# Attention with a learned distance bias and two gated layers on one core: raw rows loaded later, another grouping of the first layer, no conversions in step 0

## The chip, the cores and the metric

The kernel runs on one core of a Trainium2 chip. TensorE (PE in the profile; PEld are its weight loads) multiplies matrices, VectorE (DVE), ScalarE (ACT) and GpSimd (POOL) do the elementwise work, SyncE (SP) issues transfers between HBM and the on-chip memory. The metric is the device time of one execution in microseconds: 643.84 us, the median of three runs of the kernel before (643.73 to 643.98).

## The reference

```python
# attention: B, H, S, D = 2, 8, 576, 64
scores = q @ k.T / 8
x = log1p(|i - j|) / log1p(max(i, 1))            # of positions i, j
bias = relu(x[..., None] @ w1 + b1) @ w2         # 32 hidden, 8 heads
attn = softmax(scores + bias); a = attn @ v      # to 1152 tokens x 512
# first gated layer, 512 -> 1536 -> 512
y = (sigmoid(a @ w_gate) * (a @ w_val)) @ w_out
# second gated layer, after an RMS norm
yn = y / sqrt(mean(y * y) + 1e-6) * g
out = (silu(yn @ w_gate2) * (yn @ w_val2)) @ w_out2
```

## The kernel before, in words

Each engine runs its instructions in the order in which the program emits them; the program writes that order out by hand, as a list of actions for each turn of its loops.

**The bias.** The bias of 16 rows of positions (index T, 36 of them) is made from a table of logarithms: `bias_h` (L222) computes four hidden tiles `ht` on VectorE, ScalarE or GpSimd, `bias_mm` (L240) multiplies them by the second weights on TensorE and scales the sums into a row block `be` on ScalarE (in part on VectorE, L269), `bias_end` (L271) mirrors it and stores it to HBM (`bias_d`, on SyncE). Before the attention loop `bias_step` (L295) runs 18 times (L721) for the first 16 values of T; these are the first two tiles of positions (tile 2, then tile 1), eight values each. `load_bias` (L318) loads a block `bt` of a finished tile back, for two heads at a time; `feed_bias` (L339) does so for all units up to a number, as far as their tile is stored.

**The attention.** There are 36 units: a tile of 128 rows, a pair of heads `hp` and a batch b (the last four hold both batches). The first four are tile 2 with pairs 0, 0, 1, 1. `load_raw` (L162) loads q and k of one pair and batch in two halves of 288 KB, one per head; the first pair's and second pair's second halves go through ScalarE's queue, all others through SyncE's. In the kernel before the first two pairs (eight halves) are loaded ahead of all bias work (L192). For unit n, turn n of the loop at L732 takes the scores and bias together with their minimum (`reduce_min`, L370, VectorE), the exponential (`expo`, L389, ScalarE), the normalisation; three turns later come the transposes (L419) and the products with v (L454, `pv`).

**The gated layers.** The 1536 hidden values are 12 blocks f, the tokens three chunks c of 384. A step is one (layer, group, chunk, block); `GROUPS` says how many blocks form a group. Within a group the order is chunk by chunk, and for each chunk all blocks of the group. There are 72 steps. In turn s of the loop at L808 the program emits `gate_val(s)` (two products of 12 matmuls, `gv`, then the sigmoid `sg` on ScalarE, the product `g` on VectorE, its rounded copy `gh` on ScalarE), conversion steps, `low_part(s)` (`gl`, VectorE), `out_mm(s-2)` (12 matmuls into an accumulator `acc`) and more conversion steps. gate_val(0) is emitted earlier, in turn 36 of the attention loop. When a chunk's last block of a group is done, `collect` (L589) brings the accumulator's four parts to `part`: in a layer's first group two copies each on ScalarE and VectorE (L597, L595), in later ones four additions on VectorE (L593). The next chunk's first `out_mm` (the head) reuses that accumulator and waits for it.

**The weights** (72 pieces: gate, value and output of each block and layer) come as 512 KB transfers and are converted to two 32-bit parts, in four steps each (`piece_step`, L516): steps 0, 1, 2 and 3 have one VectorE instruction each (L522, L531, L535, L540), steps 0 and 2 have ScalarE instructions as well, step 1 an addition on GpSimd (L532). `advance(limit, micro)` emits up to `micro` such steps. In the gated loop `pace(s)` (L679) chooses how many: at least 5, up to 8 if a piece's first use comes soon. From turn 22 of the attention loop one conversion step is emitted per turn (`C`), and in the turns from 36 to 39 three.

**The norm** of the second layer runs for each chunk in four stages, one per step (`norm_stage`, L617), from the step in which the chunk's last `out_mm` of layer one is emitted; stage 3 ends with four scalings (L658) and four subtractions (L662) on VectorE, and the second layer's first step on that chunk needs them.

Of the kernel before, what the change touches and what calls it, by code (L numbers as in the profile page):

```python
# [17 lines left out]
B, H, S, D = 2, 8, 576, 64  # L18
# [5 lines left out]
CH = 384  # L24
NCH = NT // CH

GROUPS = ((2, 3, 3, 4), (4, 4, 4))
RING, EARLY, MORE = 24, 7, 7
TL = 3
WARM = 11  # L30
# [53 lines left out]
def groups_of(it):  # L84
    a, r = BLK[it]
    return range(a // 16, (a + r) // 16)
# [11 lines left out]
def fused_kernel(ctx: ExitStack, tc: tile.TileContext, qk, vp, tab, pcol, invp, prm, wts, rg, out):  # L98
    nc = tc.nc
# [58 lines left out]
    def half(b, h):  # L158
        x = (h + b) % 2 * 64
        return slice(x, x + 64)  # L160

    def load_raw(b, hp):  # L162
        t = wk.tile([128, 2, S], F32, tag=f"raw{hp // 2}", name=f"raw{b}{hp}", bufs=4)
        raws[b, hp] = t
        for h in range(2):
            r = half(b, h)
            q = nc.scalar if h and hp < 2 else nc.sync
            q.dma_start(t[r], qk[b, hp][:, r, h].rearrange("w p s -> p w s"))

    vs = {}  # L170
# [15 lines left out]
    def drain(q, k=99):  # L186
        while q and k:
            q.pop(0)()
            k -= 1

    nc.sync.dma_start(w1l[:, PARTS[1]], tab[:, PARTS[1]])
    for hp in range(2):  # L192
        for b in range(B):
            load_raw(b, hp)
    nc.sync.dma_start(w1l[:, PARTS[2]], tab[:, PARTS[2]])
    nc.sync.dma_start(w1l[:, PARTS[3]], tab[:, PARTS[3]])
    nc.gpsimd.tensor_scalar(nbpc, bpr, prms[:, 1:2], -1.0, op0=ALU.mult, op1=ALU.mult)
# [5 lines left out]
    def table(i):  # L203
        x = w1l[:, PARTS[i]]
        nc.vector.tensor_scalar(x, x, prms[:, 0:1], None, op0=ALU.mult)
# [89 lines left out]
    def bias_step(more=True):  # L295
        bias_rest()
        m, e = mq[:1], eq[:1]
        if hq and more:
            T = hq.pop(0)
            bias_h(T, *BIAS_H[GORDER.index(T)])  # L300
            mq.append(T)
        for T in m:
            bias_mm(mq.pop(0))
            eq.append(T)
        for T in e:
            bias_end(eq.pop(0))
        if eq and GORDER.index(eq[0]) < AT_ONCE:
            bias_end(eq.pop(0))
# [6 lines left out]
    NU = len(UNITS)  # L315
    st = {}

    def load_bias(n):  # L318
        b, hp, it = UNITS[n]
        bt = wk.tile([128, 2, S], F32, tag="bt", name=f"bt{n}", bufs=3)  # L320

        w = bias_width(it)
        r = rows_of(it)
        flat = bias_d[it].rearrange("a w -> (a w)")
        for h in range(2 if b is None else 1):
            o = r - 1 + (2 * hp + h) * w
            rows = flat[o : o + r * (H * w - 1)].rearrange("(i k) -> i k", k=H * w - 1)
            if b is None:
                nc.sync.dma_start(bt[h * 64 : h * 64 + 64, 0], rows[:, :S])
            else:  # L330
                nc.sync.dma_start(bt, rows[:, : 2 * w].rearrange("i (a k) -> i a k", a=2)[:, :, :S])
        st[n, "bt"] = bt
        if b is not None:
            st[n + 1, "bt"] = bt
# [4 lines left out]
    def feed_bias(last, wait=0):  # L339
        while ahead and ahead[0] <= last:  # L340
            it = UNITS[ahead[0]][2]
            seen = stored[: len(stored) - wait]
            if any(T not in seen for T in groups_of(it)):
                return
            load_bias(ahead.pop(0))
# [131 lines left out]
    def members(l, g):  # L477
        a = sum(GROUPS[l][:g])
        return range(a, a + GROUPS[l][g])

    STEPS = [
        (l, g, c, f) for l in range(2) for g in range(len(GROUPS[l])) for c in range(NCH) for f in members(l, g)
    ]
# [88 lines left out]
    def out_mm(s):  # L572
# [3 lines left out]
        head, last = f == members(l, g)[0], f == members(l, g)[-1]  # L576
        final = g == len(GROUPS[l]) - 1
        if head:
# [93 lines left out]
    def deadline(k):  # L672
        return USES[PIECES[k][:2]][0]

    def closing(s):
        return 0 <= s < NS - 1 and STEPS[s][:3] != STEPS[s + 1][:3]


    def pace(s):  # L679
        need, begun = 5, done[0] + done[1] + done[2] - 3 * done[3]  # L680
        for k in range(done[3], min(NPC, done[3] + RING)):
            todo = 4 * (k + 1 - done[3]) - begun
            need = max(need, -(-todo // max(1, deadline(k) - s - 1)))
        return min(need, 8)
# [36 lines left out]
    for i in range(PRE + 2):  # L721
        bias_step(i < PRE)
        if i == 3:
            table(1)
        if i == 9:
            feed_bias(2)
            qk_mm(0)
        if i == 12:
            table(2)
            table(3)  # L730

    for n in range(NU + TL + 1):  # L732
        if n == NU:
            attn.close()
            open_ring("me", range(EARLY, EARLY + MORE), "left")
        ev = []
        turn = (n - TL + 1) % 2
        on_dve = (1,) if n < NBIAS or n >= NU else (1,3,4)

        def evac(i):  # L740
            if len(ev) > i:
                if i in on_dve:
                    nc.vector.tensor_copy(*ev[i])
                else:
                    nc.scalar.activation(*ev[i], AF.Copy)

        def load_new():
            if n in LOADR:
                load_raw(*LOADR[n])
            if n in LOADV:  # L750
                load_v(*LOADV[n])
            if n in LASTV:
                load_last(*LASTV[n])

        live = n < NU
        nb = BSTEPS.get(n, 0)
        acts = {
            "M0": lambda: live and reduce_min(n, 0),
            "M1": lambda: live and reduce_min(n, 1),
            "X0": lambda: live and expo(n, 0),  # L760
            "X1": lambda: live and expo(n, 1),
            "T": lambda: 0 <= n - TL < NU and ev.extend(transp(n - TL)),
            "E3": lambda: evac(3),
            "E4": lambda: evac(4),
            "E0": lambda: evac(0),
            "E1": lambda: evac(1),
            "E2": lambda: evac(2),
            "N": lambda: 0 <= n - 1 < NU and normal(n - 1),
            "C": lambda: n >= NBIAS + LAG and advance(EARLY if live else EARLY + MORE, 1 if live else 2),
            "B": lambda: live and feed_bias(n + 4),  # L770
            "D": bias_rest,
            "A": lambda: nb > 1 and bias_step(),
            "c": lambda: nb > 2 and bias_step(),
            "b": lambda: nb and bias_step(),
            "L": load_new,
            "Q": lambda: n + 1 < NU and qk_mm(n + 1),
            "P0": lambda: drain(peq, 5),
            "P1": lambda: drain(peq, 5),
            "V": lambda: 0 <= n - TL < NU and [pv(UNITS[n - TL + i]) for i in range(2)],
        }  # L780
        for x in ORDERS["bias" if n < NBIAS else "late" if live else "end"][turn].split():
            acts[x]()
        if n == NBIAS - 1:
            assert not eq
            prod.close()
            open_ring("mc", range(EARLY), "right")
            fetch()
        if n >= NU:
            advance(EARLY + MORE, 1)
        if n == NU:  # L790
            while (0, 0, 1) not in wp:
                advance(EARLY + MORE, 1)
            gate_val(0)
# [14 lines left out]
    for s in range(NS + 2):  # L808
        while s < NS and (STEPS[s][0], STEPS[s][3], 1) not in wp:
            advance(done[3] + 1, 1)  # L810
        if 0 < s < NS:
            gate_val(s)
        micro = pace(s)
        if any(q[0] <= s for q in norm_queue):
            micro = min(micro, 2)

        parts = (0, micro) if closing(s - 2) else (micro // 2, micro - micro // 2)
        for half in range(2):
            k = done[3]
            if k < NPC:  # L820
                lim = k
                while lim < NPC and lim < k + 3 and (lim < RING or released(lim - RING) <= s):
                    lim += 1
                advance(lim, parts[half])
            if half == 0:
                if s < NS and not closing(s - 2):
                    low_part(s)
                if s > 1:
                    l, _, _, f = STEPS[s - 2]
                    while (l, f, 2) not in wp:  # L830
                        advance(done[3] + 1, 1)
                    out_mm(s - 2)
                if closing(s - 2):
                    low_part(s)
                while norm_queue and norm_queue[0][0] <= s:
                    _, c, stage, box = norm_queue.pop(0)
                    norm_stage(c, stage, box)
                    if stage < 3:
                        norm_queue.append([s + 1, c, stage + 1, box])
# [68 lines left out]
```

## Time and profile before

| | before |
|---|---|
| median of three runs | 643.84 us |
| profiled execution | 646.62 us |
| its span, first to last instruction | 644.8 us |
| TensorE busy | 631.2 us |
| VectorE busy | 486.2 us |
| ScalarE busy | 350.9 us |
| GpSimd busy | 214.4 us |
| mean granted TensorE clock | 0.995 |

Times in the rows below are microseconds from the first instruction of that one execution. Bias and attention take the first 175 us; the gated steps follow, some 6.27 us each in the steady state. The span is 1.8 us shorter than the execution, and the execution 2.8 us longer than the median of the runs without a profile.

### The profile page before, as it was taken

To read this page: it belongs to the slowest core of one execution; us is meant where nothing else is said; L and a number is where in the kernel's file an instruction comes from. 1 tells how busy PE (TensorE), PEld (TensorE's weight loads), DVE (VectorE), ACT (ScalarE), POOL (GpSimd) and SP (SyncE) were. 2 spreads that over 40 slices of the span, in tenths; PEclk is the share of its full clock that TensorE was granted. 3 is DMA by queue.
4 is the path that set the end of the run, shared out by engine and by line. 5 is a ranking of instruction groups with operands and counts; after the bars stand their busy time and mean duration, and the time that the engine had idled before them with its cause. 6 is when DMAs were issued, how large, how long until landed. Compare 5 with 4: busy or idle time off the path is not lost.

```text
span 644.8 us, 11729 instructions
## 1 busy us (share of the span) xinstructions
PE 631.2 (98%) x4450; PEld 575.3 (89%) x4450; DVE 486.2 (75%) x954; ACT 350.9 (54%) x745; POOL 214.4 (33%) x237
## 2 busy tenths in 40 slices
PE   9789999999998999999999999999999999999997
PEld 4246767788898999999999999999999999999997
DVE  7898898699869898888987889777877888431322
ACT  5768888988875554455543636444545445111110
POOL 6301777576753332323323221020322423100000
PEclk9999999999999999999999999999999999999999
DMA  8876956754234332343332422121433322000111
GB/s 196 293 250 199 226 187 189 261 151 131 79 94 129 103 110 91 97 132 101 116 95 82 131 65 63 38 67 33 131 99 100 109 87 66 0 1 1 50 49 50
DMA packets 28472, 71.73 MB, mean 111 GB/s; under 512 B 3840, under 2 KB 6912, under 8 KB 28416
## 3 DMA queue, kind: packets, MB, share of 16 engines
q1 hardware_dynamic: 26688, 68.41, 35.2%
q10 hardware_dynamic: 1728, 2.58, 1.4%
q8 instruction: 35, 0.57, 0.4%
q14 instruction: 21, 0.17, 0.1%
HBM read 57.72 MB, written 13.25 MB: 110 GB/s over the span
## 4 chain that ended last, share of the span: by engine, by line
PE 92%; DVE 3%; ACT 2%; DMA 2%; issue 0%; SPq 0%
PE gv L555 47%; PE s L360 6%; PE tp L419 5%; PE pv L454 5%; PE bps L253 4%; DMA bias_d<-be 1%; DVE ht L235 1%; PE pvNone L454 1%; DVE t L370 1%; PE acc122a L585 1%; DMA bt<-bias_d 1%; PE acc102b L585 1%; PE acc100b L585 1%; PE acc121b L585 1%; PE acc101b L585 1%; PE acc120b L585 1%
## 5 line engine op out<-in xcount | busy, mean ns | idle before, releaser
L532 POOL TENSOR_TENSOR ff<-ff,wr 128x512 int32<-128x512 int32 x72 | 113.9, 1582 | 260.0 <-DVE ff L531 132.9
L561 DVE TENSOR_TENSOR g<-gv,sg 128x384 f32<-128x384 f32 x72 | 40.1, 557 | 91.3 <-PE gv L555 77.2
L563 ACT ACTIVATE gh<-g 128x384 fp32r<-128x384 f32 x72 | 37.8, 525 | 99.4 <-DVE g L561 99.4
L555 PE MATMUL gv<-xh,wh 128*128 128x384 f32 x216 | 73.1, 339 | 0.0
L555 PE MATMUL gv<-xl,wh 128*128 128x384 f32 x216 | 72.8, 337 | 0.0
L555 PE MATMUL gv<-xh,wl 128*128 128x384 f32 x216 | 72.8, 337 | 0.0
L555 PE MATMUL gv<-nh,wv 128*128 128x384 f32 x240 | 64.1, 336 | 0.0
L522 DVE TENSOR_SCALAR ff<-wr 128x512 uint32<-128x512 uint32 x72 | 63.4, 881 | 0.0
L389 ACT ACTIVATE p<-t,mn 128x576 f32<-128x576 f32 x72 | 55.4, 769 | 12.7 <-DVE mn L370 12.6
L403 POOL TENSOR_SCALAR p<-p,rs 128x576 f32<-128x576 f32 x60 | 52.0, 879 | 24.3 <-PE tp L419 9.6
L370 DVE CUSTOM_DVE_ANT_0 t<-s,bt 128x576 f32<-128x576 f32 x72 | 51.6, 755 | 10.9 <-PE s L360 7.5
L559 ACT ACTIVATE sg<-gv 128x384 f32<-128x384 f32 x72 | 34.5, 480 | 44.8 <-PE gv L555 44.8
L536 ACT ACTIVATE wh<-ab 128x512 fp32r<-128x512 f32 x42 | 26.5, 632 | 56.2 <-DVE ab L535 55.8
L360 PE MATMUL s<-raw 64*128 64x288 f32 (+1 forms) x320 | 48.5, 432 | 4.1 <-DVE mn L370 4.0
L235 DVE TENSOR_SCALAR ht<-w1l,bpc 128x304 f32<-128x304 f32 (+17 forms) x100 | 51.7, 580 | 0.1
L535 DVE SCALAR_TENSOR_TENSOR ab<-ab,ff 128x512 f32<-128x512 f32 x72 | 49.0, 681 | 3.2 <-POOL ff L532 3.2
L569 DVE TENSOR_TENSOR gl<-g,gh 128x384 fp32r<-128x384 f32 x72 | 45.3, 629 | 7.0 <-ACT gh L563 7.0
L531 DVE SCALAR_TENSOR_TENSOR ff<-wr,ff 128x512 uint32<-128x512 uint32 x72 | 50.3, 699 | 0.0
L555 PE MATMUL gv<-nh,wh 128*128 128x384 f32 x144 | 48.7, 338 | 0.0
L555 PE MATMUL gv<-nl,wh 128*128 128x384 f32 x144 | 48.6, 337 | 0.0
L555 PE MATMUL gv<-nh,wl 128*128 128x384 f32 x144 | 48.6, 337 | 0.0
L525 ACT ACTIVATE wr<-wr 128x512 int32<-128x512 uint32 x72 | 48.2, 669 | 0.0
(423 smaller groups left out, 1578.7 us busy)
## 6 DMA issues: line engine op xcount, KB each, us to landing
wr<-wts SPq DMA_DIRECT2D x72, 512.0 KB, 3.6
bias_d<-be SPq DMA_DIRECT2D x36, 295.5 KB, 5.0
bt<-bias_d SPq DMA_DIRECT2D x16, 576.0 KB, 5.4
raw<-qk SPq DMA_DIRECT2D x12, 288.0 KB, 8.0
v<-vp SPq DMA_DIRECT2D x8, 320.0 KB, 4.1
raw<-qk ACTq DMA_DIRECT2D x4, 288.0 KB, 8.7
bt<-bias_d SPq DMA_DIRECT2D x8, 144.0 KB, 3.3
out<-part SPq DMA_DIRECT2D x6, 192.0 KB, 1.8
```

Source lines behind the costliest of these rows:

```text
L235: nc.vector.tensor_scalar(ht, src, bpc[:, t : t + 1], 0.0, op0=ALU.add, op1=ALU.max)
L360: nc.tensor.matmul(dst[:, hf, :288], raw[r, 0, r0 : r0 + rows], raw[r, 1, cs], start=True, stop=True)
L370: nc.vector.tensor_tensor_reduce(t, sp[:, :, :288], bt[:, 0 if UNITS[n][0] is None else j].rearrange("p (a c) -> p a c", a=2), -SCALE, 3.0e38,
L389: nc.scalar.activation(p[:, j], t.rearrange("p a c -> p (a c)"), AF.Exp, bias=mn[:, j : j + 1], scale=-1.0, accum_out=sm[:, j : j + 1],)
L403: nc.gpsimd.tensor_scalar(p[:, j], p[:, j], rs[:, j : j + 1], 1.0, op0=ALU.mult, op1=ALU.mult)
L522: nc.vector.tensor_scalar(ff, hw, 3, 0x3FFFFFFF, op0=ALU.logical_shift_left, op1=ALU.bitwise_and)
L525: nc.scalar.activation(lw.bitcast(I32), lw, AF.Copy, scale=2.0**-29)
L531: nc.vector.scalar_tensor_tensor(ff, hw, 0xC0000000, ff, op0=ALU.bitwise_and, op1=ALU.bitwise_or)
L532: nc.gpsimd.tensor_tensor(ff.bitcast(I32), ff.bitcast(I32), lw.bitcast(I32), op=ALU.add)
L535: nc.vector.scalar_tensor_tensor(ab, ab, TINY_HI, ff.bitcast(F32), op0=ALU.is_ge, op1=ALU.mult)
L555: nc.tensor.matmul(ps[:, :CH], wt[:, cs], xt[:, cc, :], start=(k == 0), stop=(k == 11))
L569: nc.vector.tensor_tensor(gl, g32, gh.bitcast(F32), op=ALU.subtract)
```

## The change

The first layer's 12 blocks are grouped 2, 2, 2, 3, 3 instead of 2, 3, 3, 4. The second pair's raw rows (four halves) are no longer loaded at the beginning but in the tenth turn of the first bias loop, behind the first bias block and before the second; both their halves go through SyncE's queue. The attention loop has one turn less at its end (n = 39, in which nothing but conversion steps is emitted). In step 0 of the gated loop no conversion steps are emitted.

```diff
-GROUPS = ((2, 3, 3, 4), (4, 4, 4))
+GROUPS = ((2,2,2,3,3), (4, 4, 4))
...
-            q = nc.scalar if h and hp < 2 else nc.sync
+            q = nc.scalar if h and hp < 1 else nc.sync
...
-    for hp in range(2):
-        for b in range(B):
-            load_raw(b, hp)
+    for b in range(B):
+        load_raw(b, 0)
...
         if i == 9:
+            feed_bias(0)
+            load_raw(0, 1)
+            load_raw(1, 1)
             feed_bias(2)
             qk_mm(0)
...
-    for n in range(NU + TL + 1):
+    for n in range(NU + TL):
...
-        micro = pace(s)
+        micro = pace(s) if s else 0
```

## Rows read from the trace of the kernel before

**Rows 1.** The page, part 1: busy time of each engine, share, instructions.
```profile
PE 631.2 (98%) x4450; PEld 575.3 (89%) x4450; DVE 486.2 (75%) x954; ACT 350.9 (54%) x745; POOL 214.4 (33%) x237
```

**Rows 2.** TensorE's waits, whole span: us in total, times, longest.
```profile
PE s L360 <- DVE mn L370: 4.0, 2, 3.1
...
```

**Rows 3.** TensorE's waits from 62 us to the end: all.
```profile
PE acc001a L585 <- ACT part L597: 2.5, 1, 2.5
```

**Rows 4.** Chain that ended last, 15 to 33 us: start, us, what.
```profile
18.16 6.22 DMA bias_d<-be
...
24.46 4.32 DMA bt<-bias_d
...
```

**Rows 5.** VectorE's timeline, 18 to 29 us: start, us, instruction, [idle before].
```profile
22.91 2.77 DVE L235 TENSOR_SCALAR ht<-w1l,bpc 128x368 f32<-128x368 f32 x7
28.80 0.76 DVE L370 CUSTOM_DVE_ANT_0 t<-s,bt 128x576 f32<-128x576 f32 x1 [3.12 <-DMA bt<-bias_d]
```

**Rows 6.** SyncE's waits, 0 to 30 us.
```profile
SPq L287 <- DMA raw<-qk: 5.7, 4, 2.7
...
```

**Rows 7.** SyncE's timeline, 8 to 40 us (issues; us are those of issuing).
```profile
10.14 9.85 SPq L287 DMA_DIRECT2D bias_d<-be  x9
24.46 0.89 SPq L331 DMA_DIRECT2D bt<-bias_d  x2
...
36.70 0.37 SPq L331 DMA_DIRECT2D bt<-bias_d  x1
...
```

**Rows 8.** Windows: us, busy PE, PEld, DVE, ACT, POOL, PEclk, DMA share, GB/s.
```profile
8.00:16.00 8.00, 7.89 (x54) 2.25 (x50) 8.00 (x17) 6.51 (x15) 6.95 (x11) 1.00 1.07 221
...
```

**Rows 9.** ScalarE's timeline, 24.5 to 34.5 us.
```profile
27.62 0.41 ACT L281 ACTIVATE be<-be 128x255 f32<-128x255 f32 x1
29.60 0.77 ACT L389 ACTIVATE p<-t,mn 128x576 f32<-128x576 f32 x1 [1.56 <-DVE mn L370]
...
```

**Rows 10.** VectorE's timeline, 29.4 to 62 us.
```profile
34.36 0.58 DVE L269 TENSOR_SCALAR be<-bps,nip,corr 128x288 f32<-128x288 f32 x1 [0.20 <-PE bps L253]
...
36.09 0.16 DVE L396 TENSOR_SCALAR sm<-sm 128x2 f32<-128x2 f32 x1
...
51.69 0.75 DVE L370 CUSTOM_DVE_ANT_0 t<-s,bt 128x576 f32<-128x576 f32 x1
...
```

**Rows 11.** TensorE's timeline, 205 to 212.5 us.
```profile
207.78 0.57 PE L585 MATMUL acc001a<-gh,wh 128*128 128x384 f32 x1 [2.45 <-ACT part L597]
...
```

**Rows 12.** Windows around that wait, columns as in rows 8.
```profile
203.50:205.30 1.80, 1.80 (x11) 1.50 (x9) 1.80 (x4) 0.49 (x1) 0.00 (x0) 1.00 0.54 98
...
207.80:211.35 3.55, 3.55 (x12) 3.55 (x13) 3.46 (x8) 2.20 (x5) 1.27 (x1) 0.52 0.48 149
...
```

**Rows 13.** Chain that ended last, 170 to 212 us.
```profile
184.17 8.52 PE gv L555 x48
...
201.09 4.26 PE gv L555 x24
...
206.97 0.77 ACT part L597 x2
...
```

**Rows 14.** VectorE's timeline, 179 to 196 us.
```profile
184.77 0.55 DVE L522 TENSOR_SCALAR ff<-wr 128x512 uint32<-128x512 uint32 x1
...
189.36 1.54 DVE L522 TENSOR_SCALAR ff<-wr 128x512 uint32<-128x512 uint32 x1
...
194.54 0.54 DVE L561 TENSOR_TENSOR g<-gv,sg 128x384 f32<-128x384 f32 x1
...
```

**Rows 15.** Windows of three steps each; the highest and lowest of four.
```profile
286.95:305.80 18.85, 18.85 (x110) 18.85 (x110) 16.43 (x26) 9.54 (x19) 6.30 (x4) 1.00 0.39 112
305.80:324.60 18.80, 18.80 (x109) 18.80 (x109) 15.91 (x26) 9.82 (x20) 4.97 (x3) 1.00 0.36 112
```

**Rows 16.** Line 593's instructions: ns min/median/max, first and last start.
```profile
L593 DVE TENSOR_TENSOR part<-acc010a,part x2: 547/552/558, 248.9 to 249.9; 128x384 f32<-128x384 f32 x2
...
```

**Rows 17.** Line 658's instructions, as in rows 16.
```profile
L658 DVE SCALAR_TENSOR_TENSOR part<-part,rgs,rb x12: 606/608/615, 389.1 to 443.6; 128x384 f32<-128x384 f32 x12
...
```

## The prediction

> **What bounds the kernel now.** The page's busy line first: TensorE is busy 631.2 of 644.8 us [rows 1]. No instruction of TensorE is added or removed by the change, so all it can win is inside the other 13.6 us, and it loses wherever it makes TensorE wait anew. So the next view is TensorE's waits. Over the whole span the largest is for the minimum of the scores, 4.0 us in two waits, both in the first 62 us [rows 2]. From 62 us to the end there is one wait only: 2.45 us at the second chunk of the first gated group [rows 3]. These are the two places that the change can touch; behind each I go back along the chain.
>
> *The start.* The chain in order of time shows the last store of the first bias tile under way from 18.16 for 6.22 us, the load of the first bias block from 24.46 for 4.32 us [rows 4], and VectorE, which ended its hidden-layer work at 22.91 + 2.77 = 25.68, idle for 3.12 us until that block landed [rows 5]. SyncE's waits say why the stores were late: four issues of stores waited 5.7 us in all until raw q/k rows had landed [rows 6]. From there to 62 us VectorE paces the kernel (it has hardly a gap, the first later one being 0.20 us [rows 10]), so time won ahead of it is time won at the end.
>
> *The stall.* TensorE stood 2.45 us before the first product of out_mm(2), until ScalarE had copied the first chunk's sums out [rows 11, 13]. Its clock was 1.00 (the 2.4 GHz level) before and 0.52 (near the 1.2 GHz level) for 3.55 us after [rows 12]. The copies were late because sigmoid and product of the gated steps ran late: the 48 matmuls of gate steps 1 and 2 ended at 184.17 + 8.52 = 192.69, so step 1's half ended near 188.4, but VectorE took up its product at 194.54 [rows 13, 14], 6.1 us late. In between it worked on conversions.
>
> **The change part by part.**
>
> *Second pair's raw rows moved.* Eight half loads of 288 KB stood ahead of the stores; four leave. At 221 GB/s, which the chip moved in 8 to 16 us [rows 8], a half takes 294,912 B / 221 GB/s = 1.33 us, so 5.3 us of transfer leave the queue ahead of the stores. What is late next is the stores' own data: nine stores stand before the first bias load in SyncE's order, and the ninth was issued by 10.14 + 9.85 = 19.99 [rows 7]; its data come from VectorE and TensorE, which the loads do not hold. So the bias load issues near 20.0 instead of 24.46. With its 4.32 us [rows 4] it lands at 24.3, and VectorE wants it at 25.68: the 3.12 us go, with 1.4 us of cover.
>
> The next limit is ScalarE: it is busy with bias rows until 27.62 + 0.41 = 28.03 and begins the first exponential at 29.60 [rows 9], so that one comes only 1.56 us sooner. VectorE's first use of it, at 36.09 [rows 10], is some 4 us behind the end of the pair (29.60, two exponentials of 0.77 and a hidden tile, about 32), so this does not pace it. The 0.20 us wait for the second half of a bias row may grow a little, as ScalarE makes one of the hidden tiles ahead of it. Bounds: 1.56 us (ScalarE paces) to 3.12 us (nothing does). I take 2.9, near the upper one, since the VectorE row is the one on the path.
>
> What is added behind: four raw halves on SyncE instead of two on each queue, 4 x 1.33 = 5.3 us of transfer between the first bias block (24.3) and the second, which then lands some 2.7 us on (589,824 B / 221 GB/s), near 32.3. The second pair is first wanted by VectorE after its 36.09 step, less 2.9. Seven stores of the second tile follow; its first bias load, issued at 36.70 [rows 7], slips by about 1 us, while its user stands at 51.69 [rows 10], now 48.8. Both are covered by over 1 and 6 us. If the first cover were gone, the loss would be what is late, up to the gain.
>
> *Rule and row on this order.* The first bias load took 4.32 us although another block and seven stores were issued right behind it [rows 4, 7]. The Trainium skill, "DMA: Bandwidth & Descriptors", section "Queues, rings and completion order", says that one queue's descriptors are consumed in ring order on each DMA engine, while different queues take turns. By that, raw halves on SyncE's own queue stay behind the bias block, as in the sum; had they shared turns with it, the block would land as in the second rival.
>
> *No conversions in step 0, and one loop turn less.* Walking the planner: the last turn (n = 39) emits three conversion steps, step 0 emits five (pace 5). All eight stand ahead of gate step 1's product on VectorE. In the trace this is all between 184.77 + 0.55 = 185.32 and 194.54, 9.2 us, with one low part in it [rows 14]. Without them VectorE does low_part(0) (0.55 us) and is free at about 185.9, before gate step 1 ends (188.4): product 1 moves from 194.54 to about 188.5. Then step 1's conversions run, five as now: c5.2, c6.1, low part, c5.3, c7.0, c6.2 (cK.i is piece_step(K, i)). At about 0.55 us each and one blocked beside GpSimd (1.54 [rows 14]) that is 4.5 us, to about 193.5, so product 2 is 1 us late rather than 7.8. Step 2 takes 4 us, product 3 waits for its gate step, and the copies, two on each engine, follow out_mm(1) at once. That ended at 201.09, where gate step 4 starts [rows 13]; the copies end near 202 and TensorE wants them at 205.3. The wait goes, with 3 us of cover. Weight pieces: step 1 needs piece 4, converted at n = 38; out_mm(1) needs piece 5, now finished in step 1.
>
> Worth: 2.45 us, and the clock. 3.55 us at 0.52 instead of 1.00 lost 3.55 x (1 - 0.52) = 1.7 us [rows 12]; with no idle ahead I let that go too. Bounds: 0 (stall moves to another head), 2.45 (clock falls anyway), 4.15. I take 4.1.
>
> *Groups of 2, 2, 2, 3, 3.* What it gives: weights of hidden blocks 2 to 4 are due in steps 6 and 12, not 6 to 8, so the planner's pace stays at 5 although eight conversion steps are missing; walked with the old groups it would be 7 in step 1 and 6 in steps 2 to 6. What it costs: 15 chunk ends instead of 12, three more with four adds of 0.55 us [rows 16] = 6.6 us of VectorE in all, beside TensorE. Room: in four stretches of three gate steps (18.85 us) VectorE was busy 15.9 to 16.4 [rows 15]. Less four adds of 0.5 us a step is 4.7, so two steps with a chunk end need 2 x 4.7 + 2.1 = 11.5 of 12.55 us. It fits, with 1 us to spare. Adds are done 2.0 us after their first, and the next chunk's first product stands one gate step (4.2 us) behind: no wait. Cost 0; bound 6 us and clock losses (third rival).
>
> The norm of chunk 0 now ends at step 34 (32 before), of chunk 1 at 37 (36), in the same steps as adds. After step 34's gate: adds to +3.7, low part 4.2, four scalings of 0.61 us at 0.53 spacing [rows 17] 6.3, first low half 6.9, the last near 8.4. Gate step 36 starts after out_mm(32), gate step 35 and out_mm(33): 2.1 + 4.2 + 2.1 = 8.4 (12, 24 and 12 matmuls at 4.26 us for 24 [rows 13]), and wants the last low half some 1.6 us later still. Cover 1.5 us; cost 0, bound 3 us.
>
> **Sum.** 2.9 + 4.1 = 7.0 us. The profiled execution took 646.62 us (span 644.8, 1.8 around it), so it would be 639.6; the median of the runs shown is 2.78 us below it, 643.84 - 7.0 = **636.8 us**.
>
> **Rivals.**
> 1. *Only the start wins.* Conversions left out at step 0 come back at once and an accumulator head at steps 4 to 8 waits as long as before: 643.84 - 2.9 = 640.9. For it: VectorE is some 85% busy [rows 15]. Against: it starts 6 us earlier and the pace does not rise.
> 2. *The bias block shares the DMA engines with the raw halves behind it*: 576 + 4 x 288 KB = 1.77 MB at 221 GB/s [rows 8] from 20.0 land near 28.0, so VectorE waits 2.3 of its 3.12 us: the start wins 0.8, the stall 4.1. Time 643.84 - 4.9 = 638.9. Against: [rows 4].
> 3. *Slower: VectorE overruns in the groups of two.* Six chunk ends in a row, steps 9 to 19. If two of the two steps' ten conversions are blocked once more beside GpSimd (1.54 instead of 0.6, 0.94 each [rows 14]), two steps need 13.4 instead of 11.5, each of the six heads waits 0.85 us and pays up to the 1.7 of the clock: 15.3 us. 643.84 - 7.0 + 15.3 = 652.1. It decides from 1.2 us a head. Against: the 1 us to spare.
> 4. *Norm and adds collide at step 36*: 1 to 3 us with the clock, 638.8 at 2.
>
> **How the numbers follow.** Forecast 0.62 (its own range 635.3 to 638.0), rival 1 0.10, rival 2 0.10, rival 3 0.08, rival 4 0.10. The range 634.9 to 641.2 holds the forecast and rivals 1, 2 and 4 but for their tails. 0.2% is 1.3 us, about what can be told from no change. Forecast and rivals 1, 2, 4 are faster; rival 3 is slower in some three quarters of its cases; some tail lies within 0.2%: faster 0.88, same 0.05, slower 0.07.
>
> **What would show it.** VectorE's first score reduction near 25.7 without idle; first bias load issued near 20 and landed before 25.7; no wait of TensorE at acc001a, clock 1.00 around it; product 1 right behind its gate step; no TensorE wait in gate steps 4 to 40. Wrong if any accumulator head of groups 1 to 3 waits, if gate step 36 waits for the norm, or if VectorE still idles at its first reduction.

## The result and the profile after

The kernel after takes 639.35 us (median of four runs, 639.07 to 639.89). The kernel before, on the same chip, took 643.91 (643.73 to 646.45). The ratio is 0.9912, 95% interval 0.9894 to 0.993: faster by 0.9%, some 5.7 us. The two medians as they stand differ by 4.6 us only, as three of the four executions of the kernel before lie at the low end of its range; side by side in a later comparison, with nine executions of the kernel before, the medians are 645.15 and 639.46, which is the same ratio and 5.7 us. The forecast was 636.8 (634.9 to 641.2). The profiled execution took 639.07 us, span 637.3, against 646.62 before: 7.55 us less, where the sum had 7.0.

The page's busy line after, and then TensorE's waits over the whole span (us in total, times, longest):

```profile
PE 628.4 (99%) x4450; PEld 573.7 (90%) x4450; DVE 490.4 (77%) x966; ACT 349.6 (55%) x745; POOL 215.9 (34%) x237
```

```profile
PE warm L143 <- DVE corr L129: 1.1, 1, 1.1
PE bps L252 <- DVE ht L234: 0.9, 2, 0.6
PE s L359 <- DVE mn L369: 0.9, 1, 0.9
...
```

TensorE has as many instructions as before [rows 1] and VectorE 12 more, the additions of three more chunk ends. The wait for the minimum of the scores fell from 4.0 us [rows 2] to 0.9, and no wait at acc001a [rows 3] is left. Line numbers up to the bias loop are one lower than before.

*The start.* SyncE's timeline after (start, us of issuing, instruction, count), and the summary of the tile `bt` from 18 to 45 us, which has the times from issue to landing of its four loads:

```profile
8.84 10.56 SPq L286 DMA_DIRECT2D bias_d<-be  x9
20.68 0.37 SPq L330 DMA_DIRECT2D bt<-bias_d  x1
21.11 2.78 SPq L168 DMA_DIRECT2D raw<-qk  x4
23.93 0.60 SPq L330 DMA_DIRECT2D bt<-bias_d  x1
...
38.60 0.37 SPq L330 DMA_DIRECT2D bt<-bias_d  x1
...
```

```profile
DMA to landing us min/median/max: 3.9/5.6/7.6
```

The first bias load is issued at 20.68 instead of 24.46 [rows 7]. It is the quickest of the four, 3.9 us, and lands at 24.6. What SyncE waited for up to 30 us says why:

```profile
SPq L286 <- ACT be L280: 10.7, 9, 3.7
SPq L286 <- DMA raw<-qk: 2.0, 2, 1.1
...
```

The wait of the stores for raw rows is 2.0 us instead of 5.7 [rows 6]; the rest is for the stores' own data. In the trace of the kernel before each of the stores held by raw rows waits for the semaphore that it then uses itself and that a raw load used last: the program's transfers take a few semaphores in turn, so such a store can't be issued until that load has landed. Fewer loads ahead of the stores mean fewer such waits. VectorE's timeline answers to [rows 5] and [rows 10] (start, us, instruction, [idle before it]):

```profile
22.87 2.76 DVE L234 TENSOR_SCALAR ht<-w1l,bpc 128x368 f32<-128x368 f32 x7
25.66 0.76 DVE L369 CUSTOM_DVE_ANT_0 t<-s,bt 128x576 f32<-128x576 f32 x1
...
30.93 0.57 DVE L268 TENSOR_SCALAR be<-bps,nip,corr 128x288 f32<-128x288 f32 x1
...
48.26 0.75 DVE L369 CUSTOM_DVE_ANT_0 t<-s,bt 128x576 f32<-128x576 f32 x1
...
```

The first reduction follows without idle, 3.1 us sooner. The bias half row at 30.93 has no idle before it either: the 0.20 us of [rows 10] went as well, so the unit at 51.69 [rows 10] now stands at 48.26, 3.43 us sooner. The windows explain that extra 0.3 us. First before, then after (columns as in [rows 8]; the clock is the column of 0.54 to 1.00):

```profile
30.00:32.00 2.00, 2.00 (x8) 1.07 (x6) 2.00 (x7) 2.00 (x6) 0.00 (x0) 0.61 1.04 409
32.00:34.00 2.00, 2.00 (x17) 0.73 (x20) 2.00 (x5) 0.81 (x2) 0.00 (x0) 0.54 1.04 388
...
```

```profile
26.00:30.00 4.00, 3.50 (x29) 1.42 (x26) 4.00 (x11) 3.94 (x9) 0.00 (x0) 1.00 1.05 213
30.00:34.00 4.00, 3.76 (x50) 1.61 (x42) 3.93 (x13) 4.00 (x11) 0.63 (x2) 1.00 1.04 386
...
```

Before, TensorE stood behind the late bias block and was granted 0.54 to 0.61 from 30 to 34 us, so the bias product that VectorE wanted came late; after, it is near the 2.4 GHz level throughout.

*The stall.* VectorE's timeline after, where [rows 14] stood, then ScalarE's copies and TensorE's next head, then the windows around the place of [rows 12]:

```profile
185.18 0.56 DVE L560 TENSOR_TENSOR g<-gv,sg 128x384 f32<-128x384 f32 x1 [2.72 <-PE gv L554]
...
191.15 0.56 DVE L560 TENSOR_TENSOR g<-gv,sg 128x384 f32<-128x384 f32 x1 [1.07 <-ACT sg L558]
...
196.52 0.56 DVE L560 TENSOR_TENSOR g<-gv,sg 128x384 f32<-128x384 f32 x1 [0.48 <-ACT sg L558]
197.68 1.02 DVE L594 COPY part<-acc000b 128x384 f32<-128x384 f32 x2 [0.61 <-PE acc000b L584]
...
```

```profile
197.54 0.85 ACT L596 ACTIVATE part<-acc000a 128x384 f32<-128x384 f32 x2
...
```

```profile
201.72 0.34 PE L584 MATMUL acc001a<-gh,wh 128*128 128x384 f32 x1
...
```

```profile
200.00:205.00 5.00, 5.00 (x30) 5.00 (x29) 4.90 (x9) 3.41 (x7) 1.84 (x1) 1.00 0.16 60
205.00:210.00 5.00, 5.00 (x31) 5.00 (x30) 2.85 (x4) 2.18 (x5) 1.64 (x1) 1.00 0.57 184
210.00:215.00 5.00, 5.00 (x30) 5.00 (x29) 4.58 (x7) 2.43 (x5) 1.83 (x1) 1.00 0.02 9
...
```

VectorE now waits for gate step 1, where it was 6.1 us late before. The copies end at 197.68 + 1.02 = 198.70, 3.0 us ahead of the head at 201.72. TensorE is busy in the whole 15 us, at 1.00. Taking the start of each gate step in both traces, the two differ by 3.44 us up to gate step 4, by 7.72 behind the stall, and by 7.59 from step 40 to the end; so the stall gave 4.27 and the new place of the norm cost 0.13.

### The profile page after: what moved, and what is told of

Same layout as the page of the kernel before. It is cut to its first block, busy times and chain, and to the rows that moved or that the text cites. A ratio compares the mean times of both kernels' runs of the same rounds, so it can differ in the third digit from the quotient of the medians.

```text
span 637.3 us, 11745 instructions
## 1 busy us (share of the span) xinstructions
PE 628.4 (99%) x4450; PEld 573.7 (90%) x4450; DVE 490.4 (77%) x966; ACT 349.6 (55%) x745; POOL 215.9 (34%) x237
## 4 chain that ended last, share of the span: by engine, by line
PE 91%; DVE 5%; ACT 2%; issue 1%; DMA 0%; SPq 0%; DVEq 0%
PE gv L554 47%; PE s L359 6%; PE tp L418 5%; PE pv L453 5%; DVE ht L234 3%; PE bps L252 3%; ACT p L388 1%; PE pvNone L453 1%; PE acc122a L584 1%; PE acc102b L584 1%; PE acc100b L584 1%; PE acc121b L584 1%; PE acc101b L584 1%; PE acc120b L584 1%; PE acc111b L584 1%; PE acc112b L584 1%
## 5 line engine op out<-in xcount | busy, mean ns | idle before, releaser
L388 ACT ACTIVATE p<-t,mn 128x576 f32<-128x576 f32 x72 | 55.3, 768 | 10.2 <-DVE mn L369 10.1
L558 ACT ACTIVATE sg<-gv 128x384 f32<-128x384 f32 x72 | 34.5, 479 | 43.4 <-PE gv L554 43.3
L568 DVE TENSOR_TENSOR gl<-g,gh 128x384 fp32r<-128x384 f32 x72 | 47.6, 661 | 5.8 <-ACT gh L562 5.8
```

The source lines that it names most:

```text
L388: nc.scalar.activation(p[:, j], t.rearrange("p a c -> p (a c)"), AF.Exp, bias=mn[:, j : j + 1], scale=-1.0, accum_out=sm[:, j : j + 1],)
```

## Experiments

The theory is of two separate gains, the start by the order of the loads and the stall by VectorE's conversions left out ahead of gate step 1, with the grouping holding the planner's pace down. The rivals are that the gain is of one part alone, that the grouping does it by itself, or that the clock carries most of it. The first question, however, was why the medians differ by less than the two profiled executions.

**The kernel before, once more** (no edit).

> The kernel before, unchanged. Its profiled execution took 646.62 us, the median of its runs is 643.84. Theory A (the stall in the gated layers is cheaper in the common executions): the times fall into two groups, near 643.8 and near 646.5, and a trace of the first group shows less than 4.1 us for the wait at acc001a and the matmuls behind it, most likely a clock of 1.00 behind it (-1.7 us). Theory B (the common executions lose less at the start): such a trace differs ahead of 62 us, with less than 3.12 us of idle before VectorE's first score reduction. Theory C (a slower profiled execution only): all times lie near 643.8, and the trace again shows both losses in full.

Measured: 644.02 us, ratio 0.9991 (0.998 to 1.0002); over the runs of the kernel before on that chip 645.19 (643.48 to 645.96, 24 runs). Its trace has the same wait, here on TensorE's timeline and in the windows:

```profile
208.27 0.45 PE L585 MATMUL acc001a<-gh,wh 128*128 128x384 f32 x1 [2.46 <-ACT part L597]
```

```profile
200.00:205.00 5.00, 5.00 (x31) 5.00 (x30) 4.02 (x6) 2.59 (x5) 1.64 (x1) 1.00 0.26 90
205.00:210.00 5.00, 2.54 (x15) 2.22 (x14) 4.52 (x10) 3.57 (x8) 1.28 (x1) 1.00 0.64 197
210.00:215.00 5.00, 5.00 (x30) 5.00 (x29) 4.90 (x9) 4.15 (x9) 2.33 (x2) 1.00 0.32 102
...
```

The wait is as long as in [rows 11], but the clock stays at 1.00 behind it, so the 1.7 us of [rows 12] are not lost in every execution. This execution (645.61 us) lost its clock at the start instead:

```profile
28.00:32.00 4.00, 2.42 (x8) 1.80 (x8) 3.24 (x9) 2.62 (x7) 0.00 (x0) 0.66 0.99 327
32.00:36.00 4.00, 4.00 (x34) 1.38 (x32) 3.43 (x9) 2.70 (x6) 0.22 (x1) 0.50 0.91 338
...
```

The mean granted clock of every execution tells the two groups that theory A expected apart: the seven of these twelve with 1.00 took 643.31 to 644.02 us, the five with 0.995 took 644.77 to 646.30; of the 24 beside them six had 1.00 (643.48 to 644.58) and 18 had 0.995 or 0.997 (644.48 to 645.96). So most executions of the kernel before have a low clock somewhere; whether at the start or at the stall, the mean does not tell. The median of a few depends on how many of either group they hold.

**The loads alone moved.** The kernel before with

```diff
-            q = nc.scalar if h and hp < 2 else nc.sync
+            q = nc.scalar if h and hp < 1 else nc.sync
-    for hp in range(2):
-        for b in range(B):
-            load_raw(b, hp)
+    for b in range(B):
+        load_raw(b, 0)
...
+            feed_bias(0)
+            load_raw(0, 1)
+            load_raw(1, 1)
             feed_bias(2)
```

> Only the second pair's raw rows moved behind the first bias block; groups, conversions and turns as before. In the trace all theories: VectorE's first score reduction near 25.7 us, gate step 0 about 3.4 us earlier, the wait of 2.45 us at acc001a stays. Median against before: theories A and C -3.4 us (640.4), theory B about -0.7 us (643.1).

Measured: 643.34 us, ratio 0.9965 (0.9953 to 0.9977), some 2.3 us. The chain and VectorE's timeline at the start, and the windows at the stall:

```profile
17.11 3.42 DMA bias_d<-be
20.65 5.70 DMA bt<-bias_d
```

```profile
26.37 0.76 DVE L369 CUSTOM_DVE_ANT_0 t<-s,bt 128x576 f32<-128x576 f32 x1 [0.56 <-DMA bt<-bias_d]
...
```

```profile
200.00:205.00 5.00, 2.86 (x17) 2.53 (x15) 4.52 (x8) 2.29 (x6) 2.12 (x2) 1.00 0.35 105
205.00:210.00 5.00, 4.80 (x19) 4.80 (x20) 4.90 (x9) 3.64 (x8) 1.83 (x1) 0.66 0.33 108
...
```

The last store takes 3.42 us instead of 6.22 [rows 4], and the bias load is issued at 20.65. Here it took 5.70 us where the kernel after had 3.9 in the same order, so VectorE still stood 0.56 us. That is one straggler: of the sixteen completion signals (updates of its semaphore) of this block in the trace fifteen had come by 24.68 us (all sixteen by 24.59 in the kernel after), the last at 26.35. In six more traces with this order, those of the last six runs below, the block took 4.1 to 4.7 us and VectorE did not wait for it. The stall stayed (2.3 us) and the clock fell behind it: the loads have no part in it. Four of the six executions have a mean clock of 0.997, as this one, and took 643.26 to 643.96 us; the two with 1.00 took 641.93 and 642.16.

**The gated part alone.** The kernel before with

```diff
-GROUPS = ((2, 3, 3, 4), (4, 4, 4))
+GROUPS = ((2,2,2,3,3), (4, 4, 4))
-    for n in range(NU + TL + 1):
+    for n in range(NU + TL):
-        micro = pace(s)
+        micro = pace(s) if s else 0
```

> Groups 2, 2, 2, 3, 3, one turn less, no conversions in step 0; raw rows as before. Trace: first score reduction at 28.8 us as before, no wait at acc001a, clock 1.00 there. Median against before: theory A -1.5 us (642.3), theories B and C -4.2 us (639.6).

Measured: 641.8 us, ratio 0.9945 (0.9934 to 0.9957), some 3.5 us. No TensorE wait is left behind 62 us. The two parts, 2.3 and 3.5, add up to the 5.7 of the whole change. Its start, which is that of the kernel before, shows how that varies:

```profile
27.33 0.76 DVE L370 CUSTOM_DVE_ANT_0 t<-s,bt 128x576 f32<-128x576 f32 x1 [1.53 <-DMA bt<-bias_d]
...
```

That wait was 3.12 us in [rows 5]; in four other traces with the old order it was 2.93, 2.85, 2.40 and here 1.53.

**The grouping alone** (the first line of that diff).

> Only the groups 2, 2, 2, 3, 3. My account: the eight conversion steps still stand ahead of gate step 1's product, so the wait at acc001a stays (2.45 us in the trace), and the three more chunk ends cost nothing: median within 0.5 us of before. Rival (the groups remove the stall by themselves): -1.5 to -4.2 us. Rival (more chunk ends cost VectorE time that TensorE waits for): slower, with waits at accumulator heads in gate steps 9 to 19.

Measured: 645.25 us, ratio 1.0 (0.9991 to 1.001). The wait at acc001a is there, 2.3 us, and the clock stays at 1.00 behind it:

```profile
205.00:210.00 5.00, 2.67 (x16) 2.57 (x16) 4.43 (x10) 3.85 (x9) 1.55 (x2) 1.00 0.53 175
...
```

By itself the grouping gives nothing and costs nothing that shows within the 0.6 us of this interval: the twelve more additions, on which the third rival rests, have room on VectorE, and no accumulator head waits in gate steps 9 to 19.

**The pause alone.** The kernel before with the shorter loop and no conversions in step 0, and the old groups.

> Old groups 2, 3, 3, 4, with one turn less and no conversions in step 0; raw rows as before. My account (the groups are what makes the pause free): blocks 2 to 4 are due in steps 6 to 8, the planner's pace rises to 7 in step 1 and 6 in steps 2 to 6, so the wait at the second chunk's head goes but TensorE waits at the heads of the third chunk or of the second group (out_mm 4 or 6), 0.5 to 2 us in all: median 1.5 to 3 us below before. Rival (the pause alone does it): no wait of TensorE from 62 us on, median as with groups and pause together, -3.5 us. Rival (the pause only moves the stall): as before.

Measured: 641.99 us, ratio 0.9953 (0.9939 to 0.9966), some 3.0 us. TensorE's only wait from 62 to 600 us, and the window that holds it:

```profile
PE acc010a L585 <- ACT part L597: 0.3, 1, 0.3
```

```profile
230.00:235.00 5.00, 4.67 (x27) 4.63 (x27) 4.53 (x7) 2.47 (x5) 2.25 (x2) 1.00 0.25 53
...
```

So the pause does most of the gated gain, and a small part comes back: without the grouping the pace rises after step 0, products run 3.7 to 4.7 us behind their gate steps in steps 5 to 8, and the head of the second group waits 0.3 us. With the grouping this wait is gone. The times alone do not tell my account from the rival that the pause does it alone, as the interval (2.2 to 3.9 us) holds both; the trace does, by that wait.

**The raw halves on two queues.** The kernel before with the loads moved, but the second halves still on ScalarE's queue (that line of the diff undone).

> Second pair's raw rows behind the first bias block as in the changed kernel, but their second halves stay on ScalarE's queue; groups and conversions as before. Order within one queue is what protects the bias block (my account): two raw halves now take turns with it, and 2 x 288 KB at 221 GB/s are up to 2.7 us, so the block takes 5 to 7 us instead of 3.9 to 5.7, VectorE waits 0.5 to 2.5 us for it, and the start wins 0.5 to 2 us less than with all on SyncE; also ScalarE spends 1.2 us on two issues among the bias rows. Median 0.5 to 2 us above the kernel with the raw rows alone on SyncE's queue (ratio 0.9965). Rival (the order of queues is of no account): the same ratio within 0.001.

Measured: 645.58 us, ratio 1.0009 (1.0001 to 1.0018): nothing is left of the 2.3 us. ScalarE's timeline (its DMA issues), the chain, VectorE's timeline, and the two queues from 22 to 23 us (packets, MB, their time as a share of 16 engines; q1 is SyncE's queue, q10 ScalarE's):

```profile
18.72 1.29 ACTq L168 DMA_DIRECT2D raw<-qk  x2
```

```profile
17.06 3.60 DMA bias_d<-be
...
20.78 7.00 DMA bt<-bias_d
...
```

```profile
27.81 0.76 DVE L369 CUSTOM_DVE_ANT_0 t<-s,bt 128x576 f32<-128x576 f32 x1 [2.19 <-DMA bt<-bias_d]
...
```

```profile
q1 hardware_dynamic: 120, 0.25, 70.9%
q10 hardware_dynamic: 60, 0.12, 31.4%
```

The bias load is issued as early as in the kernel after, but takes 7.00 us, and VectorE waits 2.2 us for it. The part of the change that keeps both halves on SyncE's queue is as necessary as the move. ScalarE issued its halves 1.4 to 2.1 us ahead of the bias load, as nothing holds its queue behind the ninth store. By the packets of the trace they ran beside that store, whose last packet starts at 22.86 us (20.76 in the kernel after); the bias block behind it begins at 23.19 us instead of 21.69, when 209 of the 256 packets of the halves had started. So most of the delay is there before the block's first packet: it comes from the halves being ahead and sharing with the store, and little of it from taking turns with the block itself.

Against the run with the loads alone the loss is 2.8 us, where 0.5 to 2 were expected. The traced execution, 643.86 us with a clock of 1.00 throughout, is the quickest of twelve; the other eleven have mean clocks of 0.995 to 0.997 and took 645.12 to 646.30. So with the wait at the start the low clock was there more often too, which I had not priced. At the stall this trace has the wait (2.5 us) without the fall:

```profile
205.00:210.00 5.00, 3.44 (x20) 3.44 (x21) 4.90 (x11) 3.42 (x7) 1.71 (x2) 1.00 0.38 123
...
```

**Which of the two omissions.** The kernel after, first with the 40th attention turn back, then with conversions in step 0 back:

```diff
-    for n in range(NU + TL):
+    for n in range(NU + TL + 1):
```
```diff
-        micro = pace(s) if s else 0
+        micro = pace(s)
```

> The changed kernel with the 40th turn restored: its three conversion steps stand again ahead of gate step 1's product, step 0 has none. My account: they take 2 to 3 us of VectorE while it would wait anyway (2.7 us of idle ahead of product 1), so product 1 comes at most 1.5 us later and the copies keep 1.5 to 3 us of cover: no wait at acc001a, same time as the changed kernel. Rival (every conversion there counts): a wait of 0.5 to 1.5 us at acc001a.

> The changed kernel with step 0's five conversion steps restored and the turn still left out. My account: five steps, one of them blocked beside GpSimd, are 4 to 5 us in front of product 1, of which 2.7 us were idle, so product 1 is 2 to 3 us late and the copies at the second chunk's head lose 2 to 3 of their 3 us of cover: no wait at acc001a or one below 0.5 us, time within 1 us of the changed kernel. Rival (step 0's conversions are the stall): the wait comes back with 1 us or more, and with it in some executions the low clock, 1 to 4 us.

Measured: 639.32 us, ratio 0.9913 (0.99 to 0.9926), and 639.21, ratio 0.9911 (0.9898 to 0.9924). Neither has a TensorE wait behind 62 us. With the new groups either omission is enough. They leave less cover: the copies end 1.7 us and 0.85 us ahead of the head instead of 3.0. Product 1 came some 2.3 and 4.2 us later than in the kernel after, where at most 1.5 and 2 to 3 were expected; the cover took that up.

**Beyond the change.** In the kernel after VectorE should still pace the first 62 us. Two edits take work off it there: the second halves of four bias rows are scaled on ScalarE as all others are (e10), and the normalisation of three units goes to GpSimd (e11); the last run has both, and the kernel after ran beside them.

```diff
-NORM_DVE = range(6)
+NORM_DVE = range(3)
-BIAS_HALF_DVE = (0, 1, 2, 3)
+BIAS_HALF_DVE = ()
```

> The changed kernel again, as the measure for the three beside it: 0.991 of before, near 639.3 us, no wait of TensorE from 62 us on. The bias block lands 3.9 to 5.7 us after its issue, so VectorE waits 0 to 0.6 us for it.

> The changed kernel with the four half bias rows of VectorE (0.5 us each) given to ScalarE. In 26 to 58 us VectorE is busy 30.4 of 32 us, ScalarE 26.9. Theory V (VectorE still paces the start): up to 2.0 us faster than the changed kernel. Rival S (ScalarE's order paces it, as each half row stands before an exponential there): no gain or slower by up to 2.4 us. I expect V in part: 0.5 to 1.5 us faster.

> The changed kernel with the normalisations of units 3, 4 and 5 on GpSimd instead of VectorE (three times 0.95 us of VectorE; two of 0.88 us on GpSimd for each unit). Theory V: up to 2.9 us faster. Rival P (VectorE's hidden tiles are blocked while GpSimd works, as its conversions are in the gated steps): the 5.3 us of GpSimd block as much as was saved: no gain, or slower by up to 2 us. I expect between: 0.5 to 2 us faster.

> Both: half rows on ScalarE and the normalisations of units 3 to 5 on GpSimd. Theory V: the gains add, up to 4.9 us, until TensorE is busy without a gap (it has about 4 us of gaps in 26 to 62 us). Rivals S and P: the larger loss of the two runs beside it stays. I expect 1 to 3 us faster than the changed kernel.

| kernel | median us | range | ratio to before |
|---|---|---|---|
| after, again | 639.46 | 639.41 to 639.50 | 0.9912 (0.9895 to 0.9929) |
| bias halves on ScalarE | 638.25 | 638.15 to 638.80 | 0.9895 (0.9878 to 0.9912) |
| three units' norm on GpSimd | 638.01 | 637.87 to 638.39 | 0.9891 (0.9874 to 0.9907) |
| both | 636.97 | 636.85 to 637.03 | 0.9873 (0.9857 to 0.989) |

They gain 1.2, 1.45 and together 2.5 us, half or a little more of what theory V gave as its most (2.0, 2.9 and 4.9). Rivals S and P, no gain or a loss, are excluded: no execution of the three is as slow as any of the kernel after. The windows of the kernel after, in that same comparison, and of the one with both:

```profile
26.00:42.00 16.00, 13.61 (x113) 5.92 (x107) 15.86 (x43) 13.07 (x29) 1.31 (x4) 1.00 0.83 244
42.00:58.00 16.00, 15.18 (x159) 9.67 (x159) 14.52 (x43) 13.98 (x33) 2.31 (x6) 1.00 0.78 280
...
```

```profile
26.00:42.00 16.00, 13.94 (x121) 6.69 (x112) 15.68 (x43) 15.32 (x34) 1.71 (x5) 1.00 0.83 240
42.00:58.00 16.00, 16.00 (x170) 10.15 (x168) 11.86 (x37) 15.47 (x39) 6.87 (x12) 1.00 0.83 304
...
```

VectorE is busy 27.5 of 32 us instead of 30.4, and ScalarE 30.8 instead of 27.1; from 42 to 58 TensorE is never free. This version beats both kernels.

## Why the prediction came out as it did

**The mechanism** held in both places. The score reduction at 25.66 without idle (forecast near 25.7), the first bias load issued at 20.68 and landed at 24.6 (20.0 and 24.3), the second tile's load slipping from 36.70 to 38.60 under cover (1 us was forecast, 1.9 came), product 1 right behind its gate step, copies 3.0 us ahead of their head (3), no wait of TensorE in the gated steps. That the bias load was issued so near to 20.0 is in part luck: I took that time from the issue of the ninth store, but the load waits until the last store of the first bias tile has landed (24.38 before, then the load at 24.46 [rows 4]; 20.53 and 20.65 in the run with the loads alone). How long that store would still take, 3.42 us instead of 6.22, was not worked out.

**The start.** Forecast 2.9 within 1.56 to 3.12; 3.44 in the two profiled executions. The upper bound left out that TensorE's clock had been low behind the late block, which cost VectorE another 0.3 us. From the first reduction to the unit at 51.69 [rows 10] it takes 22.9 us in three traces with a low clock there, 23.3 in the first experiment's, which has it twice as long, and 22.6 to 22.7 in the seven without (the last three runs, whose start is another, left out). Of the 0.3 us, 0.20 is the wait at the bias half row, which I had expected to grow and which went. Over many executions it is less: 2.3 us in the run with the loads alone, since the old order's wait ranges from 1.5 to 3.1 us (2.6 in the mean of five traces) and the new one's from none, in seven traces of eight, to 0.6.

**The stall.** Forecast 4.1; 4.27 in the profiled pair, 3.5 (2.8 to 4.3 by its interval) in the run of the gated part alone. The term that was mis-sized is the clock's 1.7 us. Of five traces with this wait of 2.3 to 2.5 us, the clock fell in two ([rows 12] and the run with the loads alone) and stayed at 1.00 in three. From the start of gate step 4 to that of step 5 the kernel after takes 6.3 us; the three traces with the wait alone take 8.9 to 9.1 and the two with the fall 10.4 to 10.6. So the wait is worth 2.6 to 2.7 us and the fall another 1.5, in those executions that have it. In the run with the loads alone, whose trace has a low clock at this place only, four executions of six had a mean clock below 1.00 and were some 1.4 us slower; at that share the fall is worth 0.9 us on average (an estimate from these six), which with the wait gives the 3.5. I priced it at its full worth, from one execution that had it.

**No conversions in step 0.** Forecast was product 2 one us late, behind VectorE's conversions. It came 1.9 us behind its gate step, but not for them: VectorE had done them and waited 1.07 us for ScalarE's sigmoid. That either omission alone is enough, with the new groups, was not seen ahead: I walked the planner with both and did not ask whether fewer steps would do.

**The groups.** Forecast cost 0, and 0 it is (ratio 1.0). In five stretches of two gate steps, where the third rival would have had TensorE wait, VectorE is busy 10.1 to 11.8 of 12.5 to 12.7 us (11.5 was worked out); the first and the fullest:

```profile
197.65:210.29 12.64, 12.64 (x73) 12.64 (x73) 10.07 (x16) 7.76 (x16) 3.47 (x2) 1.00 0.38 126
...
248.00:260.60 12.60, 12.60 (x74) 12.60 (x74) 11.81 (x21) 6.90 (x13) 4.35 (x3) 1.00 0.37 115
...
```

The least cover of a chunk's copies or additions in these groups is 1.7 us. Their worth, by the difference of the runs with and without them (0.9945 and 0.9953, whose intervals overlap) and by the trace of the latter, is about half a microsecond.

**The norm.** Forecast 0 with 1.5 us of cover; it cost 0.13 us, and TensorE does not wait at gate step 36.

**The absolute time.** The sum of 7.0 us belonged to one execution, 646.62, which is the slowest of all that the kernel before did (643.31 to 646.62): it had both the longest bias wait of five traces and the fallen clock at both places. I subtracted it from the median of three others, 643.84, whose times are those of executions without a low clock (theirs is not on record). Of the 2.55 us between 636.8 and 639.35, 1.3 are the two terms as they are on average (5.7 instead of 7.0); the other 1.25 are the start value, since over 9 to 24 runs each the kernel before has medians of 645.1 to 645.2 (the twelve of the first experiment, seven of them with a clock of 1.00, have 644.02). From that and 5.7 one has 639.4. So the measured 639.35 lies inside the stated range of 634.9 to 641.2, but outside the forecast's own 635.3 to 638.0, and nearer to the times of rivals 2 and 4 (638.9 and 638.8), which did not happen: the range held it by the width that was given for those rivals, which is luck. The kernel after is narrow, 639.07 to 639.89, with mean clocks of 0.999 to 1.00: what varied was what the change removed.

**The rivals.** Rival 1 is excluded by the gated part alone. Rival 2 is not what happens in the kernel after, but the run with two queues shows its price when the order is lost, all of the start's gain. Rivals 3 and 4 did not occur. That the clock carries most of the gain does not hold either: by the estimate above it is 0.9 of the stall's 3.5 us.

**Rule and row.** The rule of the Trainium skill that I weighed ("DMA: Bandwidth & Descriptors", "Queues, rings and completion order") is one that the trace agrees with: with four halves behind it on the same queue the first bias block took 3.9 us, no more than the 4.32 of [rows 4], and fifteen of its sixteen signals came as early in the run with the loads alone. In the run with two queues the packets of both ran in the same microsecond (120 and 60 from 22 to 23 us), which agrees with the taking of turns; there it was mainly the ninth store that shared, as the halves were ahead of the bias block in time.

## What to carry to other kernels

Behind the load that the pacing engine waits for, put on the same queue what can come later; the same loads on another queue ran ahead and took the whole gain back. A pause in background work pays where a burst of it stands ahead of the first item of a pipeline; later deadlines, which keep the planner from making it up at once, were worth about half a microsecond more here, by the trace. Price a one-off term, above all the clock, from several executions, and subtract it from a time that contains it. The mean granted clock of each execution tells which of them had that one.

## What was not expected of the hardware

- The same wait of TensorE, 2.3 to 2.5 us at the same instruction, was followed by a granted clock of 0.52 to 0.56 for some 3.6 us in two traces and by 1.00 in three. At the start it is alike: behind waits of 1.5 to 3.1 us for the bias block the clock fell in four traces of the old order and stayed at 1.00 in the fifth, whose wait was 2.85. The Trainium skill, "TensorE: Matmul & The Clock Gate", "What's actually happening", has the granted clock set by how busy TensorE has been recently; the two outcomes here differ at equal wait, and what decides between them stays open.
- One and the same order of transfers gave the first bias block in 3.9 us in the kernel after and in 5.7 us with the loads alone moved, both issued within 0.04 us of each other. The difference is the last of sixteen completion signals, which came 1.7 us behind the fifteenth; its cause was not found.
- VectorE's conversions beside GpSimd's additions still stretch, as in [rows 14] (1.54 us): in the kernel after a subtraction that otherwise takes 0.68 us took 1.81 at 187.33, beside an addition at 187.17. It costs nothing there, as VectorE waits afterwards.
